# Early loads of three head pairs and the layout of the output weights, in attention followed by a gated feed-forward block

## The chip, the cores and the metric

The kernel runs on one core of a Trainium2 chip. The core has a matrix engine (TensorE, PE in the profile), a vector engine (VectorE, DVE), a scalar engine (ScalarE, ACT), a general engine (GpSimd, POOL) and an engine that only issues transfers (SyncE, SP). Each works through its own instructions in the order in which they were written. Transfers run on 16 DMA engines beside them. The metric is the device time of one execution, in microseconds (us).

## The reference

Attention over 8 batches of 12 heads, with 448 positions and head dimension 64, and then a feed-forward block with a gate over all 3584 tokens, with weights of 768 x 1536, 768 x 1536 and 1536 x 768:

```python
def _attn_ref(q, k, v):
    scale = 1.0 / np.sqrt(q.shape[-1])
    scores = scale * np.matmul(q, k.transpose(0, 1, 3, 2))
    scores = scores - np.max(scores, axis=-1, keepdims=True)
    attn = np.exp(scores)
    attn = attn / (np.sum(attn, axis=-1, keepdims=True) + 1e-09)
    return np.matmul(attn, v).astype(np.float32)

def _moe_ref(x, w_gate, w_val, w_out):
    g = x @ w_gate
    silu = g * (1.0 / (1.0 + np.exp(-g)))
    val = x @ w_val
    return (silu * val @ w_out).astype(np.float32)
```

The attention output, with its heads laid side by side, is the x of the feed-forward block. All inputs and the output are float32.

## The kernel before, in words

**Attention by pairs of heads.** There are 48 pairs, and the main loop runs over them in order (`pr`). `qk_half` computes the scores of half a pair, two tiles of 112 keys (or chunks) at a time (L199), and ScalarE turns each tile into exponentials E in fp16 (L206). The score tiles have two buffers in PSUM, so the score product of one tile waits until ScalarE is done with the tile two before it. `sums` (L237) and `pv` (L215) multiply E with ones and with the values for two pairs together, and `scaled` (L229) writes the product into X, the input of the feed-forward block.

**Queries and keys.** They must be turned so that the head dimension lies on partitions. Pair 0 is loaded by SyncE in fp32 (`load_qk0`, L110), cast to fp16 by VectorE and ScalarE (L153, L154) and turned by TensorE (`turn0`). The other pairs are loaded by GpSimd, whose DMA casts to fp16 on the way (`load_qk16`, L118). Pairs 1 to 10 are turned by TensorE straight from that tile (`turn`, L185), and VectorE copies the result out (L188). From pair 11 on (`NPE`), GpSimd copies the pair into another order (L156), and SyncE issues a DMA that transposes it (L159). The transpose of pair `pr + 3` is issued right behind the first half of the scores of pair `pr`. Values come in groups of three pairs (`load_v`, L127).

**Feed-forward in eight blocks.** A block has 384 or 512 tokens. `ffn1_steps` makes, for each of 12 column tiles, the gate product (L264 or L267, tile gp) and the value product (vp), with a tanh on ScalarE and two VectorE operations between them. `ffn2_steps` multiplies the result hts with the output weights: for each chunk of 128 tokens and each half of 384 output columns (`oh`), 12 matmuls sum over the 1536 inner rows into one PSUM tile op. ScalarE copies that into a staging tile osb (L320), of which there are three, and SyncE writes the finished chunk to the output with one DMA for each piece of contiguous positions, two to a chunk here (L332).

**The order.** Everything is written out by hand. Block 0 starts at pair 6 (`FIRST`); its feed-forward steps are spread over the loop by `ffn_run`, which takes steps from a list according to a time budget, so that score products, value products and feed-forward steps alternate on TensorE. The six steps of block 0's own output product are at the end of its list (`own`) and fall in pairs 11, 12 and 13, two steps to a pair. Blocks 1 and later mix the output steps of the block before them among their own.

**The weights.** GpSimd loads them, with a cast to fp16, in between the loads of q, k and v: table `wq` says at which pair. Gate and value weights come in three column pieces (384, 384 and 768 columns). The output weights come in three pieces of 512 rows, all 768 columns (`wo0` to `wo2`), one at pair 6 and two at pair 7. An output step needs all 1536 rows of its 384 columns.

Of the kernel before, what the change touches and what calls it, by code (L numbers as in the profile page):

```python
# [10 lines left out]
FP32 = mybir.dt.float32  # L11
FP16 = mybir.dt.float16
# [4 lines left out]
HS = 4096.0  # L17
# [10 lines left out]
def kernel(  # L28
# [60 lines left out]
        i = min(fb // 3, 2)  # L89
        return wgv[kind, i][:, cb, ds(fb * 128 - WSPL[i][0], 128)]  # L90

    wo = [consts.tile([128, NFB // 3, DM], FP16, name=f"wo{i}") for i in range(3)]

    raw = {}
    v16 = {}
# [7 lines left out]
        for _ in range(n):  # L103
            nc.tensor.matmul(wp[:], lhsT=warm[:, 0:128], rhs=warm[:], start=True, stop=True)

    def load_qk0():
        rq = raws.tile([P, 2, NC, D], FP32, tag="rq", bufs=RB)
        rk = raws.tile([P, 2, NC, D], FP32, tag="rk", bufs=RB)
        for dst, src in ((rq, q), (rk, k)):
            nc.sync.dma_start(dst[:], src[0, 0:2].rearrange("h (p c) d -> p h (c d)", c=NC))  # L110
        raw[0] = (rq[:], rk[:])

    def load_qk16(pr, n=2):
        q16 = raws.tile([P, 4, NC, D], FP16, tag="rq", bufs=RB, name="q16")
# [16 lines left out]

    def load_w(kind, i):
        if kind == "o":
            n = NFB // 3
            src = moe_w_out[i * n * 128 : (i + 1) * n * 128, :].rearrange("(f p) m -> p f m", p=128)
            dst = wo[i]
        else:
            src = (moe_w_gate if kind == "g" else moe_w_val)[:, ds(*WSPL[i])].rearrange(
                "(a p t) m -> t p a m", p=128, t=2
            )  # L140
            for t in range(2):
                nc.gpsimd.dma_start(wgv[kind, i][:, t::2, :], src[t])
            return
        nc.gpsimd.dma_start(dst[:], src)

    def prep(pr):
        rq, rk = raw[pr]
        if pr == 0 or pr >= NPE:
            qk16 = attp.tile([P, 2, NC, 2, D], FP16, tag="qk16", bufs=3)
            for t, src in enumerate((rq, rk)):  # L150
                dst = qk16[:, 1 - t].rearrange("p c h d -> p h c d")
                if pr == 0:
                    nc.vector.tensor_copy(dst[:, 0], src[:, 0])  # L153
                    nc.scalar.activation(dst[:, 1], src[:, 1], AF.Copy)  # L154
                else:
                    nc.gpsimd.tensor_copy(dst, src)  # L156
        qkT[pr] = attp.tile([128, 2 * NC, P], FP16, tag="qkT", name="qkT", bufs=5)
        if pr >= NPE:
            nc.sync.dma_start_transpose(  # L159
                qkT[pr][:], qk16[:].rearrange("p t c h d -> p (t c h d)")  # L160
            )
            return None

        def turn0():
            for t in range(2):
                tp = ps_s.tile([128, 2, 512], FP32, tag="s", name="tp")
                for c in range(NC):
                    for hx in range(2):
                        nc.tensor.matmul(
                            tp[ts(hx, 64), c // 2, ds(c % 2 * P, P)],  # L170
                            lhsT=qk16[:, 1 - t, c, hx],
                            rhs=ident[:],
                            start=True,
                            stop=True,
                        )
                dst = qkT[pr][:, ts(1 - t, NC)].rearrange("p (a c) q -> p a (c q)", a=2)
                nc.vector.tensor_copy(dst[:, 0], tp[:, 0, 0 : 2 * P])
                nc.scalar.activation(dst[:, 1], tp[:, 1, 0 : 2 * P], AF.Copy)

        def turn():  # L180
            tp = ps_f.tile([128, 2 * NC, 128], FP16, tag="f", name="tp")
            for t in range(2):
                for c in range(NC):
                    for hx in range(2):
                        nc.tensor.transpose(  # L185
                            tp[ts(hx, 64), (1 - t) * NC + c, 0:P], raw[pr][t][:, hx, c, :], ident[:]
                        )
            nc.vector.tensor_copy(qkT[pr][:], tp[:, :, 0:P])  # L188

        return turn if pr else turn0  # L190
# [71 lines left out]
    def mm(dst, lhsT, rhs, start, stop):  # L262
        if not tiled[0]:
            nc.tensor.matmul(dst, lhsT=lhsT, rhs=rhs, start=start, stop=stop)  # L264
            return
        for j in range(4):
            nc.tensor.matmul(  # L267
                dst[ts(j, 32), :], lhsT=lhsT[:, ts(j, 32)], rhs=rhs, start=start, stop=stop
            )

    def ffn1_steps(kk, c0, n, hts):
        for fb in range(NFB):
            gp = ps_f.tile([128, 512], FP32, tag="f")
            for cb in range(NCB):
                mm(
                    gp[:, 0:n],
                    lhsT=wslice("g", fb, cb),
                    rhs=X[kk][:, cb, ds(c0, n)],
                    start=(cb == 0),
                    stop=(cb == NCB - 1),  # L280
                )
            sg = fp.tile([128, 512], FP32, tag="sg")
            nc.scalar.activation(sg[:, 0:n], gp[:, 0:n], AF.Tanh, scale=0.5)  # L283
            yield NCB * n / 2400.0
            vp = ps_f.tile([128, 512], FP32, tag="f")
            for cb in range(NCB):
                mm(
                    vp[:, 0:n],
                    lhsT=wslice("v", fb, cb),
                    rhs=X[kk][:, cb, ds(c0, n)],  # L290
                    start=(cb == 0),
                    stop=(cb == NCB - 1),
                )
            t1 = fp.tile([128, 512], FP32, tag="t1")
            nc.vector.scalar_tensor_tensor(  # L295
                t1[:, 0:n], sg[:, 0:n], 1.0, gp[:, 0:n], ALU.add, ALU.mult
            )
            nc.vector.scalar_tensor_tensor(  # L298
                hts[:, fb, 0:n], t1[:, 0:n], 0.5 * HS, vp[:, 0:n], ALU.mult, ALU.mult
            )  # L300
            yield NCB * n / 2400.0

    def ffn2_steps(kk, c0, n, hts, last_block):
        for ch in range(n // 128):
            last = last_block and ch == n // 128 - 1
            for oh in range(2):
                if last or oh == 0:
                    osb = fp.tile([128, DM], FP32, tag="osb", bufs=3)
                parts = [(OH, OH // 2), (OH + OH // 2, OH // 2)] if last and oh else [(oh * OH, OH)]
                for m0, w in parts:  # L310
                    op = ps_f.tile([128, 512], FP32, tag="f")
                    for fb in range(NFB):
                        mm(
                            op[:, 0:w],
                            lhsT=hts[:, fb, ts(ch, 128)],
                            rhs=wo[fb // (NFB // 3)][:, fb % (NFB // 3), ds(m0, w)],
                            start=(fb == 0),
                            stop=(fb == NFB - 1),
                        )
                    nc.scalar.activation(osb[:, ds(m0, w)], op[:, 0:w], AF.Copy, scale=1.0 / HS)  # L320
                    if not last:
                        m0, w = 0, DM
                        if oh == 0:
                            continue
                    l0 = c0 + ch * 128
                    l = l0
                    while l < l0 + 128:
                        b, j = divmod(l, S)
                        c, p0 = divmod(j, P)
                        m = min(P - p0, l0 + 128 - l)  # L330
                        eng = nc.scalar if last and m < 64 else nc.sync
                        eng.dma_start(  # L332
                            out[ts(NB * kk + b, S), :].rearrange("(p c) m -> c p m", c=NC)[
                                c, p0 : p0 + m, ds(m0, w)
                            ],
                            osb[l - l0 : l - l0 + m, ds(m0, w)],
                        )
                        l += m
                yield NFB * OH / 2400.0

    def block(i):
        kk, odd = divmod(i, 2)
        c0, n = (384, 512) if odd else (0, 384)
        hts = hp_.tile([128, NFB, 512], FP16, tag="h")
        return ffn1_steps(kk, c0, n, hts), ffn2_steps(kk, c0, n, hts, i == B - 1), n

    with tc.manual_schedule():
        load_qk0()
        nc.vector.memset(warm[:], 0.0)
        nc.vector.memset(ones[:], 1.0)  # L350
        load_qk16(1, 1)
        make_identity(nc, ident)
        load_v(0, 0, 2)
        load_qk16(2, 1)
        load_v(0, 2)
        load_qk16(3, 1)
        load_qk16(4)
        load_v(1)
        dummy(6)
# [7 lines left out]
            3: [("qk", 10), ("V", 2), ("g", 2), ("v", 2)],  # L367
            4: [("qk", 12)],
            6: [("V", 3), ("o", 0)],
            7: [("o", 1), ("o", 2)],  # L370
        }

        def emit(item):
# [158 lines left out]
```

## Time and profile before

| | |
|---|---|
| time, median of 4 runs | 467.57 us (465.80 to 471.06) |
| the profiled execution's own time | 465.8 us |
| its span, first to last instruction | 463.8 us |
| TensorE matmul busy | 453.9 us (98%) |
| ScalarE busy | 243.2 us (52%) |
| VectorE busy | 236.9 us (51%) |
| GpSimd busy | 101.9 us (22%) |
| mean granted TensorE clock | 0.996 |
| read from HBM, written to it | 47.19 MB, 11.01 MB |

The busy time of TensorE is the union of its matmuls, whose ends are modelled and overlap: a long run of matmuls counts as busy throughout even where each waits a little for the one before. A row of the timeline reads: start, length, engine, line, operation, output <- inputs, number of instructions, and in brackets how long the engine was idle before it and what ended that. A row of the waits reads: who waited for whom, microseconds in total, number of times, the longest.

### The profile page before, as it was taken

The numbers are of one execution on the slowest core, as the hardware profiler recorded it, in microseconds if no ns is written. First come the engines' busy times: TensorE is split into PE (matmuls) and PEld (weight loads), VectorE is DVE, ScalarE is ACT, GpSimd is POOL, SyncE is SP. The second block draws the span as 40 slices with busy tenths as digits, with TensorE's granted clock in tenths as the row PEclk, the third lists the DMA queues.
The fourth block names the chain that finished last, engine by engine and source line by source line (L and its number), as shares of the span: only waits on it lengthen the run. The fifth ranks groups of instructions, "written<-read, shape, count | busy, mean of one in ns | idle before, by whom it ended". The sixth has DMA issues, their size and how long they took to land.

```text
span 463.8 us, 14131 instructions
## 1 busy us (share of the span) xinstructions
PE 453.9 (98%) x6367; PEld 228.0 (49%) x6367; DVE 236.9 (51%) x371; ACT 243.2 (52%) x353; POOL 101.9 (22%) x162
## 2 busy tenths in 40 slices
PE   7899989999999999999999999999999999999996
PEld 3345444444455555444455555444445556554454
DVE  2565763466764553655645635545456546334310
ACT  7887556656565555546455564546455552222222
POOL 8554407241350042202222040210200000000000
PEclk9899999999999999999999999999999999999999
DMA  9999999991994282861939675813513111101123
GB/s 142 197 199 209 174 185 197 188 166 30 110 124 62 63 112 42 131 94 28 140 40 108 95 109 95 116 31 75 90 17 55 37 37 35 36 2 34 35 68 102
DMA packets 78940, 44.23 MB, mean 95 GB/s; under 512 B 36640, under 2 KB 75424, under 8 KB 78880
## 3 DMA queue, kind: packets, MB, share of 16 engines
q0 software_dynamic: 39264, 23.37, 38.4%
q1 hardware_dynamic: 39520, 19.92, 24.6%
q8 instruction: 49, 0.80, 0.7%
q14 instruction: 11, 0.09, 0.1%
q10 hardware_dynamic: 96, 0.05, 0.0%
HBM read 47.19 MB, written 11.01 MB: 125 GB/s over the span
## 4 chain that ended last, share of the span: by engine, by line
PE 84%; DMA 13%; POOL 2%; issue 1%; ACT 0%; POOLq 0%
PE gp L267 15%; PE op L264 14%; PE vp L267 13%; PE op L267 10%; PE vp L264 9%; PE s L199 8%; PE acc L215 7%; PE gp L264 7%; DMA wo<-in_moe_w_out_dram 6%; DMA wg<-in_moe_w_gate_dram 5%; PE acc L237 4%; DMA q<-in_q_dram 2%; POOL q L118 1%; POOL k L118 0%; POOL vt L127 0%
## 5 line engine op out<-in xcount | busy, mean ns | idle before, releaser
L206 ACT ACTIVATE E<-s 112x896 f16<-112x896 f32 x192 | 164.8, 916 | 26.2 <-PE s L199 26.0
L283 ACT ACTIVATE sg<-gp 128x384 f32<-128x384 f32 (+1 forms) x96 | 52.3, 545 | 85.4 <-PE gp L267 54.7
L295 DVE SCALAR_TENSOR_TENSOR t<-sg,gp 128x384 f32<-128x384 f32 (+1 forms) x96 | 58.5, 610 | 64.3 <-ACT sg L283 64.2
L320 ACT ACTIVATE osb<-op 128x384 f32<-128x384 f32 (+1 forms) x57 | 27.7, 486 | 102.0 <-PE op L264 57.8
L267 PE MATMUL gp<-X,wg 128*32 128x512 f16 (+1 forms) x1416 | 78.1, 355 | 0.0
L252 DVE RECIPROCAL R<-ssb 128x112 f32<-128x112 f32 x92 | 73.1, 827 | 0.7
L298 DVE SCALAR_TENSOR_TENSOR hts<-t,vp 128x384 f16<-128x384 f32 (+1 forms) x96 | 59.6, 621 | 23.3 <-PE vp L267 7.9
L264 PE MATMUL op<-wo,hts 128*128 128x384 f16 (+1 forms) x408 | 68.7, 321 | 1.4 <-DMA wo<-in_moe_w_out_dram 1.4
L267 PE MATMUL vp<-X,wv 128*32 128x512 f16 (+1 forms) x1224 | 66.9, 353 | 0.0
L229 DVE TENSOR_TENSOR X<-acc,R 128x448 f16<-128x448 f32 x48 | 29.7, 624 | 66.4 <-PE acc L215 64.5
L264 PE MATMUL vp<-X,wv 128*128 128x384 f16 (+1 forms) x270 | 58.4, 352 | 0.0
L199 PE MATMUL s<-qkT 64*128 64x448 f16 x384 | 54.9, 357 | 2.4 <-ACT E L206 2.0
L264 PEld LDWEIGHTS <-hts 128*128 128x128 f16 x408 | 38.9, 98 | 29.7 <-issue 4.6
L267 PEld LDWEIGHTS <-wg 128*32 128x32 f16 x1416 | 37.8, 97 | 29.6
L267 PE MATMUL op<-wo,hts 128*32 128x384 f16 x1104 | 48.9, 326 | 0.0
L264 PE MATMUL gp<-X,wg 128*128 128x384 f16 (+1 forms) x222 | 47.4, 350 | 0.0
L215 PE MATMUL acc<-E,vt 112*32 112x448 f16 x768 | 45.5, 357 | 0.0
L267 PEld LDWEIGHTS <-wv 128*32 128x32 f16 x1224 | 32.7, 97 | 25.5
L127 POOL DMA_DIRECT2D vt<-in_v_dram x17 | 13.0, 763 | 145.5 <-PE acc L215 144.4
L264 PEld LDWEIGHTS <-wv 128*128 128x128 f16 x270 | 25.3, 98 | 26.9 <-issue 4.8
L267 PEld LDWEIGHTS <-hts 128*32 128x32 f16 x1104 | 29.5, 97 | 16.3
L156 POOL COPY qk<-q 112x512 f16<-112x512 f16 x37 | 22.9, 620 | 63.9 <-DMA qkT<-qk 47.8
(38 smaller groups left out, 199.2 us busy)
## 6 DMA issues: line engine op xcount, KB each, us to landing
vt<-in_v_dram POOLq DMA_DIRECT2D x15, 336.0 KB, 5.1
q<-in_q_dram POOLq DMA_DIRECT2D x22, 224.0 KB, 6.2
k<-in_k_dram POOLq DMA_DIRECT2D x22, 224.0 KB, 7.3
out_dram<-osb SPq DMA_DIRECT2D x7, 336.0 KB, 3.1
wo<-in_moe_w_out_dram POOLq DMA_DIRECT2D x3, 768.0 KB, 24.2
out_dram<-osb SPq DMA_DIRECT2D x8, 288.0 KB, 2.9
out_dram<-osb SPq DMA_DIRECT2D x8, 240.0 KB, 3.0
out_dram<-osb SPq DMA_DIRECT2D x8, 192.0 KB, 2.7
```

Source lines behind the costliest of these rows:

```text
L156: nc.gpsimd.tensor_copy(dst, src)
L199: nc.tensor.matmul(s[:, hx, 0:S], lhsT=t[ts(hx, 64)].rearrange("p c q -> p (c q)")[:, c * P : c * P + 128], rhs=t[ts(hx, 64), NC:, :].rear ...
L206: nc.scalar.activation(E[pr][:, c], s[0:P, :, 0:S], AF.Exp, scale=sm_scale)
L215: nc.tensor.matmul(acc[ts(j, 32), 0:S], lhsT=v16[g][:, 2 * r + j % 2, c, :].rearrange("p (d t) -> p t d", t=2)[:, t], rhs=E[p0 + j // 2][: ...
L229: nc.vector.tensor_tensor(X[kk][:, hp + t, ts(bb, S)], acc[:, 0:S], R[p0][:], ALU.mult)
L252: lambda i=i: nc.vector.reciprocal(rt[:, ts(i, P)], ssb[:, ts(i, P)]) for i in range(4)
L264: nc.tensor.matmul(dst, lhsT=lhsT, rhs=rhs, start=start, stop=stop)
L267: nc.tensor.matmul(dst[ts(j, 32), :], lhsT=lhsT[:, ts(j, 32)], rhs=rhs, start=start, stop=stop)
L283: nc.scalar.activation(sg[:, 0:n], gp[:, 0:n], AF.Tanh, scale=0.5)
L295: nc.vector.scalar_tensor_tensor(t1[:, 0:n], sg[:, 0:n], 1.0, gp[:, 0:n], ALU.add, ALU.mult)
L298: nc.vector.scalar_tensor_tensor(hts[:, fb, 0:n], t1[:, 0:n], 0.5 * HS, vp[:, 0:n], ALU.mult, ALU.mult)
L320: nc.scalar.activation(osb[:, ds(m0, w)], op[:, 0:w], AF.Copy, scale=1.0 / HS)
```

## The change

There are three edits.

1. **Pair 1.** `load_qk0` becomes `load_qk32(pr)`, and SyncE now loads pairs 0 and 1 in fp32. `prep(1)` has VectorE cast both tensors into a tile qk16 (two casts of 112 x 512), and `turn` takes pair 1 from there. GpSimd no longer issues the two loads of pair 1.
2. **Order of the first loads on GpSimd.** Before: pair 1, values of pair 0, pair 2, values of pairs 1 and 2, pair 3, pairs 4 and 5, values of group 1. After: pair 2, pair 3, all the values of group 0 in one transfer, pairs 4 and 5, values of group 1.
3. **Output weights.** Instead of three tiles of 512 rows x 768 columns there are two tiles of 1536 rows x 384 columns, one loaded at pair 6 and one at pair 7. Block 0 takes its output steps in another order: first all three chunks with the first half of the columns, then all three with the second half. Each of these six steps takes a staging tile of its own and writes its half of the columns with DMAs of its own. The other blocks keep their order and only address the weights anew.

```diff
-    wo = [consts.tile([128, NFB // 3, DM], FP16, name=f"wo{i}") for i in range(3)]
+    wo = [consts.tile([128, NFB, OH], FP16, name=f"wo{i}") for i in range(2)]
...
-    def load_qk0():
+    def load_qk32(pr):
         rq = raws.tile([P, 2, NC, D], FP32, tag="rq", bufs=RB)
         rk = raws.tile([P, 2, NC, D], FP32, tag="rk", bufs=RB)
         for dst, src in ((rq, q), (rk, k)):
-            nc.sync.dma_start(dst[:], src[0, 0:2].rearrange("h (p c) d -> p h (c d)", c=NC))
-        raw[0] = (rq[:], rk[:])
+            nc.sync.dma_start(dst[:], src[0, 2 * pr : 2 * pr + 2].rearrange("h (p c) d -> p h (c d)", c=NC))
+        raw[pr] = (rq[:], rk[:])
...
-            n = NFB // 3
-            src = moe_w_out[i * n * 128 : (i + 1) * n * 128, :].rearrange("(f p) m -> p f m", p=128)
+            src = moe_w_out[:, ts(i, OH)].rearrange("(f p) m -> p f m", p=128)
...
-        if pr == 0 or pr >= NPE:
+        if pr < 2 or pr >= NPE:
...
-                    nc.gpsimd.tensor_copy(dst, src)
+                    (nc.gpsimd if pr > 1 else nc.vector).tensor_copy(dst, src)
...
-                        nc.tensor.transpose(
-                            tp[ts(hx, 64), (1 - t) * NC + c, 0:P], raw[pr][t][:, hx, c, :], ident[:]
-                        )
+                        src = qk16[:, 1 - t, c, hx] if pr == 1 else raw[pr][t][:, hx, c, :]
+                        nc.tensor.transpose(tp[ts(hx, 64), (1 - t) * NC + c, 0:P], src, ident[:])
...
-    def ffn2_steps(kk, c0, n, hts, last_block):
-        for ch in range(n // 128):
-            last = last_block and ch == n // 128 - 1
-            for oh in range(2):
-                if last or oh == 0:
-                    osb = fp.tile([128, DM], FP32, tag="osb", bufs=3)
...
+    def ffn2_steps(kk, c0, n, hts, first, last_block):
+        chunks = range(n // 128)
+        if first:
+            steps = [(ch, oh) for oh in range(2) for ch in chunks]
+        else:
+            steps = [(ch, oh) for ch in chunks for oh in range(2)]
+        for ch, oh in steps:
+            last = first or (last_block and ch == n // 128 - 1)
+            if last or oh == 0:
+                osb = fp.tile([128, DM], FP32, tag="osb", bufs=3)
...
+                        rhs=wo[oh][:, fb, ds(m0 - oh * OH, w)],
...
-        load_qk0()
+        load_qk32(0)
+        load_qk32(1)
         nc.vector.memset(warm[:], 0.0)
         nc.vector.memset(ones[:], 1.0)
-        load_qk16(1, 1)
+        load_qk16(2, 1)
         make_identity(nc, ident)
-        load_v(0, 0, 2)
-        load_qk16(2, 1)
-        load_v(0, 2)
         load_qk16(3, 1)
+        load_v(0)
         load_qk16(4)
         load_v(1)
...
-            7: [("o", 1), ("o", 2)],
+            7: [("o", 1)],
```

More of the change, by code (lines that the diff above doesn't have):

```diff
@@ L301, in ffn1_steps @@
             yield NCB * n / 2400.0
-    def ffn2_steps(kk, c0, n, hts, last_block):
-        for ch in range(n // 128):
-            last = last_block and ch == n // 128 - 1
-            for oh in range(2):
-                if last or oh == 0:
-                    osb = fp.tile([128, DM], FP32, tag="osb", bufs=3)
[L309 to L339, printed above, removed]
@@ new lines, in ffn2_steps @@
+    def ffn2_steps(kk, c0, n, hts, first, last_block):
[8 more added lines that the diff above has]
+                osb = fp.tile([128, DM], FP32, tag="osb", bufs=3)
+            parts = [(OH, OH // 2), (OH + OH // 2, OH // 2)] if last and oh and not first else [(oh * OH, OH)]
+            for m0, w in parts:
+                op = ps_f.tile([128, 512], FP32, tag="f")
+                for fb in range(NFB):
+                    mm(
+                        op[:, 0:w],
+                        lhsT=hts[:, fb, ts(ch, 128)],
+                        rhs=wo[oh][:, fb, ds(m0 - oh * OH, w)],
+                        start=(fb == 0),
+                        stop=(fb == NFB - 1),
+                    )
+                nc.scalar.activation(osb[:, ds(m0, w)], op[:, 0:w], AF.Copy, scale=1.0 / HS)
+                if not last:
+                    m0, w = 0, DM
+                    if oh == 0:
+                        continue
+                l0 = c0 + ch * 128
+                l = l0
+                while l < l0 + 128:
+                    b, j = divmod(l, S)
+                    c, p0 = divmod(j, P)
+                    m = min(P - p0, l0 + 128 - l)
+                    eng = nc.scalar if last and m < 64 and not first else nc.sync
+                    eng.dma_start(
+                        out[ts(NB * kk + b, S), :].rearrange("(p c) m -> c p m", c=NC)[
+                            c, p0 : p0 + m, ds(m0, w)
+                        ],
+                        osb[l - l0 : l - l0 + m, ds(m0, w)],
+                    )
+                    l += m
+            yield NFB * OH / 2400.0
@@ L344, in block @@
         hts = hp_.tile([128, NFB, 512], FP16, tag="h")
-        return ffn1_steps(kk, c0, n, hts), ffn2_steps(kk, c0, n, hts, i == B - 1), n
+        return ffn1_steps(kk, c0, n, hts), ffn2_steps(kk, c0, n, hts, i == 0, i == B - 1), n
     with tc.manual_schedule():
-        load_qk0()
+        load_qk32(0)
+        load_qk32(1)
         nc.vector.memset(warm[:], 0.0)
         nc.vector.memset(ones[:], 1.0)
-        load_qk16(1, 1)
+        load_qk16(2, 1)
         make_identity(nc, ident)
-        load_v(0, 0, 2)
-        load_qk16(2, 1)
-        load_v(0, 2)
         load_qk16(3, 1)
+        load_v(0)
         load_qk16(4)
```

## The prediction

> **What bounds the kernel now.** The page's second part first.
>
> ```profile
> PE   7899989999999999999999999999999999999996
> PEclk9899999999999999999999999999999999999999
> DMA  9999999991994282861939675813513111101123
> ```
>
> A slice is 11.6 us. TensorE is full from the third slice to the last, so a stall of TensorE there costs its length, and a gain in the first 31 us is kept only if nothing later makes TensorE wait. DMA is full for nine slices, 104 us: until then transfers come when the queue gets to them, not when they are asked for. The second slice has a lower clock. The waits of TensorE are short:
>
> ```profile
> PE s L199 <- ACT E L206: 2.0, 4, 0.8
> PE op L264 <- DMA wo<-in_moe_w_out_dram: 1.4, 1, 1.4
> ...
> PE tp L185 <- DMA q<-in_q_dram: 0.4, 1, 0.4
> ...
> PE tp L185 <- DMA k<-in_k_dram: 0.2, 1, 0.2
> ```
>
> Windows of 3.41 us put the clock beside the work (length, busy, matmuls, granted clock, DMA share, GB/s):
>
> ```profile
> 10.85:14.26 3.41, 2.00 (x34) 1.00 1.40 184
> 14.26:17.67 3.41, 3.41 (x44) 0.50 1.44 198
> 65.45:68.87 3.42, 2.47 (x18) 1.00 1.19 156
> ```
>
> A window with TensorE busy for 2.00 us (59%) was followed by one at half clock, one with 2.47 us (72%) was not. Last, the timeline where block 0 projects:
>
> ```profile
> 66.45 1.46 PE L264 MATMUL op<-wo,hts 128*128 128x384 f16 x8
> 69.28 0.81 PE L264 MATMUL op<-wo,hts 128*128 128x384 f16 x4 [1.36 <-DMA wo<-in_moe_w_out_dram]
> 73.21 1.22 SPq L159 DMA_TRANSPOSE qkT<-qk  x1
> 74.48 1.04 SPq L332 DMA_DIRECT2D out_dram<-osb  x2
> 75.70 1.65 SPq L159 DMA_TRANSPOSE qkT<-qk  x1
> 80.01 1.07 SPq L332 DMA_DIRECT2D out_dram<-osb  x2
> 86.30 0.62 POOL L156 COPY qk<-q 112x512 f16<-112x512 f16 x1 [6.17 <-DMA qkT<-qk]
> 86.31 0.49 ACT L320 ACTIVATE osb<-op 128x384 f32<-128x384 f32 x1 [1.31 <-PE op L264]
> 88.86 0.55 PE L199 MATMUL s<-qkT 64*128 64x448 f16 x4
> ```
>
> Eight of the first step's twelve matmuls run on wo0 and wo1, and four wait 1.36 us for wo2. On SP a transpose (pair 14) goes out at 73.21, behind it the outputs of chunk 0, then pair 15's transpose, which lands at 86.15 (GpSimd's copy of pair 18 waits for it), then chunk 1's outputs, issued at 80.01 and 80.37, which land at 88.42 and 88.83.
>
> **Pair 1 and the order of the loads.** Gains: GpSimd issues two loads of 0.66 to 0.78 us less, and the two value loads become one, so pair 3 is issued at about 3.2 and 3.9 instead of 5.91 and 6.57. It lands at about 8.5 instead of 11.18 and 11.79, and the 0.6 us of waits at L185 go. ScalarE's idle time in front of E up to 19 us is 0.53, 0.56, 0.46 and 0.60 us. The first is that wait. The other three lie in the half-clock window, where `sums` took 1.30 us (0.94 elsewhere) and `pv` 1.29 (0.94). Without the wait the window before would be busier, and the drop probably goes: 0.5 + 1.2 = 1.7 us at most, if the drop goes; 0.5 if it stays.
>
> Costs: VectorE gets two casts of 112 x 512. Half that size took 0.39 us (L153), so one is 0.65 us by that row (0.78 doubled; 0.5 at best). VectorE is free from 5.58 to 7.27, which hides 1.3 us but for the start: the key tensor of pair 1 is fourth in SP's queue. Pair 0's two tensors landed at 3.58 and 4.28, 0.7 apart, which gives 5.7 alone and, beside GpSimd's loads, about 6.5. Its cast ends at 7.15, its transposes at 7.5 instead of 7.23, and the third score tile is 0.3 to 0.6 us late for ScalarE, whose E chain from 6.04 has no gap. I take 0.4. The start gains 1.3 us at most, 0.1 with the drop; I take 1.0. The values of group 0 are first used at 16.92 and land at about 10.5, as before: hidden, 6 us of cover. Cover gone, `pv` would wait.
>
> **Does the fp32 route relieve the DMA?** Pair 0's 448 KB moved at up to 337 GB/s, casting loads at about 200 GB/s written (400 read): 1.3 us of the engines for a pair in fp32, 1.1 us for its 224 KB with a cast. No work is saved. The Trainium skill (DMA: Bandwidth & Descriptors, "Issuing engines are not separate DMA queues") says that loads from SyncE and GpSimd share the same 16 engines and that only issue time is saved. By it the stream of loads gains nothing. But by the trace the engines were not full: values and pair 2 (112 KB each) landed at 7.11, 8.12 and 9.42, 1.0 to 1.3 us apart, and the pair 3 loads of the same size 0.6 apart. That is room of 1.6 us; I count 1.0 of it (0 to 1.6).
>
> **Output weights.** Bytes are the same, rows half as long. Gate pieces with such rows land 1.44 us per 288 KB, those with double rows 2.78 per 576: 0.05 us per 288 KB, so eight times that, 0.4 us, are lost, and one issue of 0.75 us on GpSimd is saved, which nobody waits for. The stream is then 1.0 - 0.4 = 0.6 us earlier behind the weights. The three pieces land between 56.06 and 69.24; the first half alone at about 62.5. The first step wants it at 66.45 less 1.0. The 1.36 us go. The second half is wanted by step 4 at about 75: hidden. The value weights that landed at 48.13 are wanted at 49.29 less 1.0, with 1.0 to spare: hidden as well. So TensorE would reach pair 14 some 2.4 us early.
>
> **The output stage, where a wait is added.** Six staging tiles are taken instead of three, from three buffers. Step 4, 5 and 6 copy into the buffers of steps 1, 2 and 3, so ScalarE waits for those outputs to land, and behind it on ScalarE stand the exponentials. On SP the outputs of step 1 stand behind pair 14's transpose, which waits for GpSimd's copies (SP waited 41 us in all for those before 110 us), and those of step 3 behind pair 15's. SP issues twelve outputs instead of six, 0.3 to 0.7 us each.
>
> Step 4: step 1's outputs follow the transpose, landed at 77.49 - 0.6, by some 1.5 us: 78.4. The copy is wanted at 79.49 - 2.4 = 77.1, and the scores of pair 13 tolerate about 78.4: nothing lost. Step 5: 80 or so against a tolerance of 82: nothing. Step 6 needs step 3's outputs. Pair 15's transpose landed 6.3 us after chunk 0's outputs (79.81); it follows steps 1 and 2 now, the same bytes in twice the rows: 79.8 - 0.6 + 0 to 1.5. Then step 3's two outputs, half of chunk 1's bytes, which landed up to 2.7 us after the transpose: 1.35 by bytes, 2.7 by rows. Together 86.15 - 0.6 + 0.6 + 1.7 = 87.9 (from 86.8 to 89.7).
>
> What does TensorE lose? Behind the copy on ScalarE come 0.4 us of its length and two exponentials of 0.87 us, and pair 14's second half needs the buffers of both: its last score product can go at 87.9 + 2.1 = 90.0. Before it went at 88.86 + 0.18 = 89.04. So the gain of 2.4 us is gone and about 1.0 is lost, the start's gain included, whatever it was. TensorE stands idle from about 86.5 to 90.0 but for one product. The clock: by the rows above, a window of 3.41 us with 59% of work was followed by a half-clock one. This idle time leaves one window with about 20%, or two with half. The Trainium skill (TensorE: Matmul & The Clock Gate, "Why this matters for your kernels") would only have an idle gap of over about 3 us return the clock to half, so by the rule it is at the edge: 0 or 1.7. By the row it is 3.41 / 2 = 1.7 us of lost work. I take the row. The sum is +1.0 + 1.7 = 2.7; with the transposes a little quicker, 2.3. I say +2.5.
>
> **The rivals.**
> 1. *The outputs land in time.* If pair 15's transpose takes 4.3 us as pair 14's did, not 6.3 behind outputs, or the buffers' halves are held apart, step 6 doesn't wait, and both gains stay: -1.36 - 1.0 = -2.4, with a part of the 1.8 us by which the median lies above the profiled run, which may be longer waits for wo2, up to -4. For it: pair 16's transpose took 3.3 us behind outputs. Against: the GpSimd copies show only one of three that fast in this stretch.
> 2. *The recycled buffers cost over 1%.* Transposes under full load took 11 to 16 us from issue (pairs 11 to 13). If pair 15's lands 3 us later, at 89.2, step 3's outputs land at 91; then TensorE loses 91 + 2.1 - 89.0 = 4.1 us and two windows at half clock, 3.4 less what overlaps: +6.5, 474.1. It decides from a landing at about 90.
> 3. *The edits don't reach the end:* the start is paced by E, wo2's wait moves to the next load, step 6 has just enough time: 0, 467.6. For it: the two amounts, 2.4 gained and 2.4 tolerated, are near each other.
>
> **How the numbers follow.** The sum is against the profiled execution: span 463.8, own time 465.8, the median 467.57. +2.5 makes a span of 466.3, own time 468.3, and 470.1 on the median, which is what is compared. Chances: the forecast 50%, rival 1 25%, rival 2 17%, rival 3 8%. The range takes the forecast (+0.8 to +4.5), the nearer end of rival 1 (-2.9) and most of rival 2 (+6.8): 464.7 to 474.4. One per cent, 4.7 us, is about what a measurement of this kernel can tell from no change. Faster by more: under half of rival 1, 0.11. Slower by more: nearly all of rival 2 and a quarter of the forecast, 0.29. Within: 0.60.
>
> **What would show it.** Right: no wait of op on wo; L185 no longer waits on q or k; ScalarE's osb copies of the fourth and sixth step wait for an output DMA; scores of pair 14 wait for E at about 86 to 90; then a window at half clock. The clock row around 14 us may be 1.00. Wrong: osb copies that wait only for TensorE, or the scores of pair 14 at about 86.4. The prediction falls if the drop at 14 us returns or moves between runs by more than the effect, or if output rows of 1536 bytes take as long as rows of 3072.

## The result, and the profile after

The changed kernel takes 465.96 us in the median of 43 runs (464.98 to 468.39), the one before 467.85 us in 64 runs beside it (464.84 to 471.06). The ratio is 0.9962 with a 95% interval of 0.9950 to 0.9975: 1.8 us faster, where 2.5 us slower were forecast. The fastest runs of both are nearly equal; the change mostly takes away the longer ones.

The profiled execution took 465.55 us with a span of 463.2 (before 465.8 and 463.8). The page's second part, for TensorE, its clock and the DMA:

```profile
PE   8899999999999999999999999999999999999996
PEclk9999999999999999999999999999999999999999
DMA  9999999991994373671948585813513111101123
```

The low clock in the second slice is gone. The rest of this part differs little, so the waits of TensorE come next:

```profile
PE s L197 <- ACT E L204: 1.8, 4, 0.4
PE wp L104 <- DVE ones L353: 1.2, 1, 1.2
PE tp L185 <- DVE qk L155: 0.6, 1, 0.6
PE tp L168 <- DVE qk L152: 0.5, 1, 0.5
PE acc L235 <- ACT E L204: 0.4, 1, 0.4
```

The wait of op for wo and those of L185 for q and k are gone. L185 now waits for the cast of pair 1 instead. The timeline of the start, ScalarE and VectorE:

```profile
6.86 1.73 ACT L204 ACTIVATE E<-s 112x896 f16<-112x896 f32 x2 [0.26 <-PE s L197]
7.12 0.65 DVE L155 CAST qk<-rq 112x512 f16<-112x512 f32 x1 [0.92 <-DMA rq<-in_q_dram]
...
8.51 0.43 DVE L155 CAST qk<-rk 112x512 f16<-112x512 f32 x1 [0.73 <-DMA rk<-in_k_dram]
...
10.64 1.73 ACT L204 ACTIVATE E<-s 112x896 f16<-112x896 f32 x2 [2.06 <-PE s L197]
```

The casts wait for the fp32 loads of pair 1, which land at 7.10 and 8.48 us. The chain of exponentials, which ran without a gap from 6.04 before, now stops for 2.06 us after two tiles. Block 0's first gate product starts at 32.16 instead of 31.24. From the timeline of block 0's output stage, with rows left out between these:

```profile
67.37 2.11 PE L262 MATMUL op<-wo,hts 128*128 128x384 f16 x12
72.08 1.22 SPq L158 DMA_TRANSPOSE qkT<-qk  x1
73.40 2.01 SPq L334 DMA_DIRECT2D out_dram<-osb  x4
75.59 1.73 SPq L158 DMA_TRANSPOSE qkT<-qk  x1
77.41 3.27 SPq L334 DMA_DIRECT2D out_dram<-osb  x4
78.94 0.49 ACT L322 ACTIVATE osb<-op 128x384 f32<-128x384 f32 x1 [0.48 <-PE op L262]
85.52 0.62 POOL L155 COPY qk<-q 112x512 f16<-112x512 f16 x1 [6.39 <-DMA qkT<-qk]
86.30 0.49 ACT L322 ACTIVATE osb<-op 128x384 f32<-128x384 f32 x1 [1.84 <-DMA out_dram<-osb]
88.26 0.55 PE L197 MATMUL s<-qkT 64*128 64x448 f16 x4
```

The twelve matmuls of the first step run through. Step 1's outputs do stand behind pair 14's transpose (72.08). They land at 77.72 and 78.20, so the copy of step 4, at 78.94, waits only for its product. The copy of step 6 waits 1.84 us for an output, as forecast. But the scores of pair 14's second half start at 88.26, 0.6 us earlier than before and with no wait in front of them. It was just in time: the last of these products goes at 88.46, and ScalarE had freed its buffer at 88.40.

**Three numbers for a profile.** They describe every profile of this study: G, the start of block 0's first gate product; W, from there to the scores of pair 15; and the rest. The rest is 370.4 to 370.5 us in all of them, before and after and in all variants. So whatever the edits do, they do it before pair 15, at about 93 us. W is 60.58 where TensorE waits for nothing on the way. Before: G 31.24, W 62.10. After: G 32.16, W 60.58. Between these two profiles the start lost 0.92 us, and the stretch behind it gained 1.52, of which 1.36 is the wait for wo2.

### The profile page after: what moved, and what is told of

Read it like the earlier page. It is cut to its first block, busy times and chain, and to the rows that moved or that the text cites. A ratio compares the mean times of both kernels' runs of the same rounds, so it can differ in the third digit from the quotient of the medians.

```text
span 463.2 us, 14146 instructions
## 1 busy us (share of the span) xinstructions
PE 455.0 (98%) x6367; PEld 228.4 (49%) x6367; DVE 237.9 (51%) x373; ACT 243.2 (52%) x353; POOL 99.9 (22%) x158
## 4 chain that ended last, share of the span: by engine, by line
PE 95%; ACT 2%; DMA 1%; SPq 0%; issue 0%; DVE 0%; ACTq 0%
PE gp L265 15%; PE op L262 14%; PE vp L265 13%; PE vp L262 11%; PE op L265 10%; PE s L197 10%; PE gp L262 9%; PE acc L213 9%; PE acc L235 4%; ACT E L204 2%; DMA rk<-in_k_dram 1%; PE tp L185 1%; PE wp L104 0%; SPq L110 0%; DVE qk L155 0%
## 5 line engine op out<-in xcount | busy, mean ns | idle before, releaser
L127 POOL DMA_DIRECT2D vt<-in_v_dram x16 | 12.4, 777 | 147.0 <-PE acc L213 146.4
```

## The experiments

Each was compared with runs of the kernel before on the same chip. "Time" is the ratio with its 95% interval. G, W and pair 15 come from one profiled execution each; the early version has two, and six runs for each of its two times. One more variant, six staging tiles instead of three, has no row: their pool would need 30 KB per partition, and 23.6 KB were left.

| kernel | G | W - 60.58 | pair 15 | time |
|---|---|---|---|---|
| before | 31.24 | 1.52 | 93.34 | 1 |
| before, second profile | 32.13 | 2.67 | 95.38 | |
| after | 32.16 | 0.00 | 92.74 | 0.9962 (0.9950 to 0.9975) |
| after, again | 32.90 | 0.00 | 93.48 | 0.9977 (0.9962 to 0.9992) |
| output weights alone | 32.06 | 1.43 | 94.07 | 0.9977 (0.9957 to 0.9996) |
| start alone | 32.45 | 2.00 | 95.03 | 0.9984 (0.9957 to 1.0011) |
| order of loads and output weights, no fp32 | 30.77 | 2.35 | 93.69 | 0.9981 (0.9962 to 1.0001) |
| after, a staging tile for each chunk | 33.12 | 0.00 | 93.70 | 0.9956 (0.9940 to 0.9972) |
| before, block 0 reads wo0 alone | 32.80 | 0.00 | 93.38 | 0.9957 (0.9939 to 0.9976) |
| early version | 30.64, 30.44 | 0.00, 0.04 | 91.22, 91.06 | 0.9927 (0.9899 to 0.9955), 0.9924 (0.9897 to 0.9952) |
| early version, recycled staging tiles | 29.91 | 6.39 | 96.88 | 1.0030 (1.0010 to 1.0049) |
| early version, fp32 pair 1 | 32.30 | 0.00 | 92.88 | 0.9959 (0.9945 to 0.9974) |
| the same, GpSimd's first load later | 30.84 | 0.00 | 91.42 | 0.9915 (0.9895 to 0.9935) |

**Output weights alone.** The change without its start: `load_qk0`, pair 1 by GpSimd, values as before.

```diff
-        load_qk32(0)
-        load_qk32(1)
+        load_qk0()
...
-        load_qk16(2, 1)
+        load_qk16(1, 1)
         make_identity(nc, ident)
-        load_qk16(3, 1)
-        load_v(0)
+        load_v(0, 0, 2)
+        load_qk16(2, 1)
+        load_v(0, 2)
+        load_qk16(3, 1)
```

> Only the output weights and block 0's step order are changed; the loads at the start are as before. Theory (the gain is the wait for the last third of the output weights, and the new start costs about 0.9 us): no wait of op for wo, ratio to before 0.993 to 0.995 (2.3 to 3.3 us less), that is more than the whole change. Rival (the gain comes from the start): 0.999 to 1.000. Rival of the prediction (recycled staging tiles take the gain back): TensorE arrives earlier than in the changed kernel, so the copy of step 6 waits 2.5 us or more and scores of pair 14 wait with it; ratio 0.998 to 1.003.

0.9977: less gain than my theory had (0.993 to 0.995), and just short of the range of the prediction's rival (0.998 to 1.003), which the interval overlaps. The wait for wo is gone, but another is there. Rows of the timeline of this kernel:

```profile
73.32 1.22 SPq L158 DMA_TRANSPOSE qkT<-qk  x1
...
74.59 2.00 SPq L335 DMA_DIRECT2D out_dram<-osb  x4
...
81.43 0.49 ACT L323 ACTIVATE osb<-op 128x384 f32<-128x384 f32 x1 [3.08 <-DMA out_dram<-osb]
82.78 0.37 PE L198 MATMUL s<-qkT 64*128 64x448 f16 x2 [0.62 <-ACT E L205]
...
83.59 0.37 PE L198 MATMUL s<-qkT 64*128 64x448 f16 x2 [0.44 <-ACT E L205]
```

The copy of step 4 waits 3.08 us for step 1's outputs, and the scores of pair 13 wait behind it. So the recycled tiles can reach TensorE, and not because it is early: step 1's product starts at 67.27 here and at 67.37 in the changed kernel. The outputs are late. Pair 14's transpose goes out at 73.32 instead of 72.08, and step 1's outputs land at 81.15 and 81.33 instead of 77.72 and 78.20.

**Start alone.** The change with the output weights in three pieces of rows and block 0's old order of steps.

```diff
-    wo = [consts.tile([128, NFB, OH], FP16, name=f"wo{i}") for i in range(2)]
+    wo = [consts.tile([128, NFB // 3, DM], FP16, name=f"wo{i}") for i in range(3)]
```

> Only the loads at the start are changed (pair 1 by SyncE in fp32, pairs 2 and 3 ahead of the values); output weights as before. Theory: block 0 begins 0.5 to 1 us later than before, but op's wait for wo shrinks by as much, so the end doesn't move: ratio 0.999 to 1.001. Rival (the gain comes from the start): 0.996 to 0.997.

0.9984 with 1 inside the interval, which holds the rival's 0.997 as well. In the profile G is 1.2 us later, more than the 0.5 to 1 expected, and op still waits 1.8 us for wo: the late start didn't shorten that wait as I had expected it to, since the weights were late too (70.93 instead of 69.24).

**Order and output weights, without fp32.** Pair 1 by GpSimd ahead of pair 2.

```diff
-        load_qk32(1)
+        load_qk16(1, 1)
```

> The changed kernel, but pair 1 is loaded by GpSimd with a cast, as before, ahead of pair 2. Theory: pair 1 lands at 5.5 and 6.1 instead of 7.1 and 8.5, so ScalarE's gap of 2 us in pair 0 goes, and the start is earlier than before: block 0 begins 0.5 to 1.5 us earlier than before; ratio to before 0.991 to 0.994, unless the staging tiles hold it at 0.996. Rival (the fp32 route is the gain): 0.997 to 1.000.

The start came out at the lower end of what was expected (G 30.77, 0.5 us earlier) and the time did not. The waits of TensorE say why:

```profile
PE s L198 <- ACT E L205: 2.7, 6, 0.4
PE vp L263 <- DMA wv<-in_moe_w_val_dram: 1.4, 1, 1.4
```

The last value weights landed at 50.45, where they had landed at 48.13 before, and the product that needs them was there earlier. The recycled tiles cost about 0.75 more: from pair 13 to pair 14 it took 7.57 us instead of 6.83 in the changed kernel. There too step 1's product starts where it did in the changed kernel (67.51), and its outputs land late, at 80.19 and 81.01. The ratio, 0.9981, lies in the rival's range, but its reason is not that fp32 loads start the kernel sooner: without them the start is earlier, and the value weights and the outputs land later.

**A staging tile for each chunk.** The two steps of a chunk share one, and each writes its half of the columns.

```diff
-            if last or oh == 0:
-                osb = fp.tile([128, DM], FP32, tag="osb", bufs=3)
+            if oh == 0 or (last and not first):
+                tiles[ch] = fp.tile([128, DM], FP32, tag="osb", bufs=3, name="osb")
+            osb = tiles[ch]
```

> The changed kernel, but the two steps of a chunk of block 0 share a staging tile and write its two halves, so that no copy waits for an output to land. Theory (in the changed kernel the late start leaves TensorE just the room, so the wait costs nothing when the start is late): no wait of osb copies for output DMAs; median within 0.15% of the changed kernel, at most 0.5 us better. Rival (recycled tiles cost in most runs): 0.8 us or more better than the changed kernel.

No copy waits for an output any more. The median is 465.73 us, beside 466.02 for the changed kernel on the same chip: 0.3 us. By the two ratios of the table it would be 1.0 us, but their intervals overlap. W is 60.58 in this profile and in both of the changed kernel, so in these the recycled tiles cost TensorE nothing.

**What the wait for wo2 is worth.** The kernel before, but block 0's output product reads the first third of the output weights for all its rows. It leaves out the other two thirds there, and with them the wait.

```diff
-                            rhs=wo[fb // (NFB // 3)][:, fb % (NFB // 3), ds(m0, w)],
+                            rhs=wo[0 if c0 == 0 and kk == 0 else fb // (NFB // 3)][:, fb % (NFB // 3), ds(m0, w)],
```

> The kernel before, but block 0's output steps read the first third of the output weights for all rows (the product of block 0 is left with wrong weights), so that they wait for the first third alone. It measures what the wait for the last third is worth. Theory (that wait is the gain): ratio 0.9955 to 0.997, as the whole change. Rival (the gain comes from elsewhere): 0.998 or more.

0.9957: taking the wait away alone gains as much as the whole change. The median falls by 2.6 us (467.37 to 464.73), more than the 1.36 us of the first profile. The second profile of the kernel before has the reason; this is its timeline of TensorE:

```profile
67.34 1.46 PE L264 MATMUL op<-wo,hts 128*128 128x384 f16 x8
71.32 0.81 PE L264 MATMUL op<-wo,hts 128*128 128x384 f16 x4 [2.51 <-DMA wo<-in_moe_w_out_dram]
```

> The kernel before, for a second profile. Theory (in most runs the wait for the last third of the output weights is longer than the 1.4 us of the first profile, or the start is later): block 0 between 31.2 and 33 us and op waits 1.5 to 4 us for wo, pair 15 at 60.6 us plus that wait behind it. Rival (the first profile is typical): 1.2 to 1.5 us.

2.51 us here: wo2 landed at 71.28, not at 69.24. That execution took 467.82 us, near the median; the first one, 465.8, is among the fastest quarter.

**The changed kernel again.**

> The changed kernel as it is, for the comparison on one chip: ratio to before 0.995 to 0.9975 in all theories; in its profile pair 15 begins between 92.0 and 93.5 us, and the first gate product at 31.5 to 32.5 if the fp32 loads of pair 1 land at 7 and 8.5 us again.

Pair 15 at 93.48, as expected. G is 32.90, later than expected, with the fp32 loads at 7.61 and 8.92, later than the 7 and 8.5 that the expectation assumed. W is 60.58 once more. Step 1's outputs had landed by 77.28.

**The early version.** All that the readings so far name as a limit is taken away: pair 1 by GpSimd, pairs 2 and 3 ahead of the values, output weights in halves, a staging tile for each chunk, and the values of group 2 behind the last gate and value weights:

```diff
-            3: [("qk", 10), ("V", 2), ("g", 2), ("v", 2)],
+            3: [("qk", 10), ("g", 2), ("v", 2), ("V", 2)],
```

> Pair 1 by GpSimd as before, pairs 2 and 3 ahead of the values, output weights in halves, one staging tile for each chunk in block 0, and the values of group 2 loaded behind the last gate and value weights. Theory (the start, the value weights at 48 to 50 us, the staging tiles and the output weights take turns as the limit, and none of the four holds now): block 0 begins at about 30.8 and pair 15 at about 91.3 us in the profile, 2 us earlier than in the profile of before; ratio to before 0.992 to 0.995. Rival (something else limits, the time is that of the changed kernel): 0.996 to 0.998.

> The early version with one staging tile for each chunk, again, since few of its runs counted the first time. Ratio to before 0.9905 to 0.994; block 0 at 30.5 to 31 us, pair 15 at 60.58 us behind it (the least that any profile shows), 91.1 to 91.6.

0.9927 and 0.9924, with medians of 463.71 and 463.49 us: faster than both kernels. G and pair 15 come within 0.2 us of what was expected, all on the early side.

**The recycled tiles with an early start.** The early version with the change's way of taking staging tiles.

```diff
-            if oh == 0 or (last and not first):
-                tiles[ch] = fp.tile([128, DM], FP32, tag="osb", bufs=3, name="osb")
-            osb = tiles[ch]
+            if last or oh == 0:
+                osb = fp.tile([128, DM], FP32, tag="osb", bufs=3)
```

> The early version (pair 1 by GpSimd, pairs 2 and 3 ahead of the values, output weights in halves, values of group 2 behind the last gate and value weights) with the recycled staging tiles of the change, six from three buffers, instead of one for each chunk. TensorE arrives about 2 us earlier than in the changed kernel, so this is the case that the prediction reckoned with. Theory: copies of steps 4 and 6 wait for outputs and the scores of pairs 13 and 14 with them; pair 15 begins 0.7 to 2 us later than with a tile for each chunk (91.2), at 91.9 to 93.2; ratio to before 0.994 to 0.9965. The prediction as it stood: pair 15 at about 94.3 and a window at half clock after it: ratio 0.999 to 1.002. Rival (the recycled tiles cost nothing even then): 91.0 to 91.5 and 0.992 to 0.9935.

TensorE is as early here as the prediction had reckoned with, and this kernel is the slowest: 1.0030, median 468.92. My theory at that time had the cost far too small, and the prediction's number was the nearer one. Timeline of this kernel, SP, ScalarE and TensorE:

```profile
73.38 1.22 SPq L158 DMA_TRANSPOSE qkT<-qk  x1
...
74.66 3.00 SPq L335 DMA_DIRECT2D out_dram<-osb  x4
...
81.61 0.49 ACT L323 ACTIVATE osb<-op 128x384 f32<-128x384 f32 x1 [5.41 <-DMA out_dram<-osb]
82.00 1.72 ACT L205 ACTIVATE E<-s 112x896 f16<-112x896 f32 x2
82.96 0.56 PE L198 MATMUL s<-qkT 64*128 64x448 f16 x2 [2.94 <-ACT E L205]
...
85.87 3.94 PE L263 MATMUL op<-wo,hts 128*128 128x384 f16 x12
```

Step 1's outputs are issued behind pair 14's transpose at 74.66 and land at 79.21 and 81.50. The copy of step 4 waits for them, ScalarE's exponentials wait behind the copy, and the scores of pair 13 wait for those. Then twelve matmuls take 3.94 us where they had taken 2.12. Windows of 3.41 us of this kernel, TensorE alone (length, busy, matmuls, granted clock, DMA share, GB/s), say why:

```profile
79.37:82.78 3.41, 0.65 (x4) 1.00 1.35 217
82.78:86.19 3.41, 2.98 (x22) 0.50 1.33 152
86.19:89.61 3.42, 3.42 (x12) 0.50 1.34 222
89.61:93.02 3.41, 3.41 (x50) 1.00 1.24 244
```

One window with 0.65 us of work is followed by two at half clock, worth 3.4 us. With the wait of 2.94 that makes about the 6.39 in the table.

**The fp32 route by itself.** The early version with `load_qk32(1)` as in the change.

> The same, but with pair 1 loaded by SyncE in fp32 as in the change; nothing else differs. Theory (the fp32 loads land at 7.5 and 8.9 instead of 5.7 and 6.3, and cost the start about 2 us): block 0 at 32.1 to 33.1, ratio to before 0.9945 to 0.997, and 0.0025 to 0.005 above the version with pair 1 by GpSimd. Rival (the fp32 route costs nothing in the median): within 0.001 of it.

G is 32.30 instead of 30.44 to 30.64, and the ratio 0.9959 instead of 0.9924 and 0.9927: about 0.0033, or 1.5 us in time (1.9 to 2.2 between the medians) and 1.8 in G. Loading pair 1 in fp32 costs about what the new order of the other loads gains. The same edit has a second effect: with two loads less on GpSimd, pair 14's transpose goes out at 71.45 here, and at 73.54 and 75.37 in the two profiles of the early version.

**Why the fp32 loads are late.** The same kernel, with GpSimd held back before its first load by twelve clears and by the making of the identity, which stood behind that load:

```diff
+        make_identity(nc, ident)
+        hold = consts.tile([112, 112], FP16, name="hold")
+        for _ in range(12):
+            nc.gpsimd.memset(hold[:], 0.0)
         load_qk16(2, 1)
-        make_identity(nc, ident)
```

> The early version with pair 1 in fp32 and a staging tile for each chunk, but GpSimd first clears a scratch tile twelve times (about 2 us) before it issues its first load, so that the fp32 loads of pair 1 have the DMA engines to themselves. Theory (pair 1 is late because its loads share the engines with GpSimd's): pair 1 lands at 4.9 to 6.0 instead of 7.4 and 8.7, and ScalarE's gap in pair 0 is under 0.7 us instead of 2.9. Rival (the fp32 loads are slow by themselves or by their place in SP's queue): they land at 6.8 or later and the gap stays over 1.5 us. The time says less, since all of GpSimd's loads are 2 us late: ratio to before 0.992 to 1.000.

GpSimd issues its first load at 4.17 instead of 1.3 us, and pair 1 lands at 5.89 and 6.43 instead of 7.4 and 8.7; the gap of ScalarE is 1.12 us instead of 2.92. The landings are at or near the theory's, so sharing the engines with GpSimd's loads accounts for the lateness. The gap lies between the two expectations, but what is left of it is not the loads': the same 1.12 us stands in "order and output weights, without fp32" and in the first profile of the early version, where pair 1 comes by GpSimd and lands at 5.6 to 6.3. In these three profiles TensorE's clock record begins at about 10 us, and its first matmuls run at half speed. In the second profile of the early version, with the clock up at 5.1, ScalarE has no such gap. The ratio, 0.9915, is the lowest of the study, though all of GpSimd's loads start 2.9 us later. The intervals of this and the early version overlap, so which of the two is faster stays open.

## Why the prediction was wrong

**Two terms failed: the start's gain and the landing of step 3's outputs.** The forecast's 2.5 was 1.0 of lost time and 1.7 of half clock, less a little. The 1.0 came from one landing: step 3's outputs at 87.9, and 2.1 us later, at 90.0, the last score product of pair 14. They landed at 86.19, below the whole range given (86.8 to 89.7), and that product went at 88.46, 0.6 us earlier than before. The 2.1 us from that landing to the product held within 0.2. The 1.7 needed a TensorE that stands idle, because it is 2.4 us ahead. It was 0.6 us ahead and did not wait.

**Why the start gained nothing.** The prediction put the second of pair 1's fp32 loads at "5.7 alone and, beside GpSimd's loads, about 6.5", took 0.4 us for it and 1.0 us as the gain of the start. The two landed at 7.10 and 8.48, and in four other profiles with this start at 7.4 to 8.9. Its bound from below had been 0.1 us of gain; a loss was left out, though the next paragraph has the two streams on the same engines. GpSimd's loads were slowed as well: pair 2 landed at 6.94 and 8.30. How much was lost is less certain than the 0.92 us of the first two profiles:

| loads at the start | G in four profiles | mean |
|---|---|---|
| as before | 31.24, 32.06, 32.13, 32.80 | 32.06 |
| as in the change | 32.16, 32.45, 32.90, 33.12 | 32.66 |
| the change's order, pair 1 by GpSimd | 29.91, 30.44, 30.64, 30.77 | 30.44 |

The first profile of before is the earliest of its four. A gain of 1.0 is not there. The means differ by 0.6, a loss, and the two rows overlap. The fp32 route costs 2.2 us by the last two rows, which do not overlap. A slow clock at the start is not the reason: in two profiles with the fp32 loads (the change with a tile for each chunk, the early version with fp32) the clock came up at 5.3 and 5.6 us, though it fell again at 8.7 and 9.1, and ScalarE's gap was 3.12 and 2.92 us all the same.

**The mechanism that was to cost 2.5 us is real, and what spared the changed kernel was the time at which its outputs landed.** Five profiles have recycled tiles:

| kernel | step 1 starts | pair 14's transpose issued | step 1's outputs landed by | cost |
|---|---|---|---|---|
| after | 67.37 | 72.08 | 78.20 | 0 |
| after, again | 68.11 | 71.14 | 77.28 | 0 |
| output weights alone | 67.27 | 73.32 | 81.33 | 1.43 |
| order and output weights, no fp32 | 67.51 | 73.77 | 81.01 | 0.75 |
| early version, recycled | 65.12 | 73.38 | 81.50 | 6.39 |

At step 4 the forecast of 78.4 and "nothing lost" was right for the change. The third and fourth row have TensorE where the first has it, and pay, because their outputs land 3 us later. The fourth differs from the changed kernel in the route of pair 1 alone (its value weights cost it another 1.4, earlier); its pair 14 keys, for which the transpose waits, landed at 73.07 instead of 71.39. So the edit that took the gain from the start also brought pair 14's transpose and the outputs behind it forward. The prediction had this as 0.6 us in the stream of loads; it had not seen that step 4 hangs on it. Two things stay open: why the late outputs also took longer from issue to landing (4.6 to 6.6 us instead of 4.2 to 4.4), and why the start alone, with the weights in three pieces, did not bring the transpose forward (74.89). With TensorE 2 us earlier still (the last row) the chain ran as described: outputs behind a transpose, copy, exponentials, scores, half clock, for 5 to 6 us. It did so at step 4, where the prediction had seen no cost. At step 6 the changed kernel had 0.06 us of room, 0.15 in its second profile: that nothing waited there is luck.

**Other terms of the sum.**
- Step 3's outputs: forecast 87.9, measured 85.81 and 86.19. They came 0.4 and 0.8 us behind pair 15's transpose (85.38), not 1.7. The fear of the shorter rows was not borne out there.
- The wait for wo2: mis-sized for the median. It was 1.36 us in the first profile, 2.51 in the second, 2.6 in the median by the kernel that needs wo0 alone. The prediction allowed for that under its first rival only and compared with the median all the same.
- The stream of loads: forecast 0.6 us earlier behind the weights. The second half landed at 69.57, wo2 had landed at 69.24; but pair 14's tensors behind it landed at 70.23 and 71.39 instead of 71.10 and 72.51, about 1 us earlier. By the Trainium skill's rule (DMA: Bandwidth & Descriptors, "Issuing engines are not separate DMA queues") nothing was to be gained there. At the start the rule fits: the two streams slowed each other.
- The first half: forecast 62.5, measured 60.65, wanted at 67.37. Right. Edits hidden as said: the values of group 0 landed at 11.34, wanted at 18.19.
- The last value weights "with 1.0 to spare": 49.29 less 1.0 less 48.13 is 0.16, so the 1.0 stands only with the room counted above. They landed at 48.59 and nothing waited, but with an earlier start they were the next limit, 1.4 us.
- VectorE's casts: forecast 0.65 each, measured 0.65 and 0.43, right.
- The clock: the row taken as a rule, half clock behind a window with 59% of work, does not hold alone. In the second profile of before, a window with 1.88 us of work in 3.42 (55%, from 69.78) was followed by one at full clock. One with 19% was followed by two at half clock in the early version with recycled tiles; the 1.7 us was too small by half for that case. The other rule weighed there (the Trainium skill, TensorE: Matmul & The Clock Gate, "Why this matters for your kernels", over about 3 us of idle) agrees with both: the waits were 2.51 and 2.94 us, the second at its edge. It does not explain the window of 59%, in which no gap was over 0.9 us. In the changed kernel no such window came.
- What a measurement can tell: the interval of the result is 0.25% wide, so 0.4% stands out from no change, where the prediction had put the limit at about one per cent.
- One of the three idle times laid to the half-clock window at the start ends at 18.55, behind that window's end at 17.67.

**The rivals.** The first one, that both gains stay, gave -2.4 to -4 and was nearest to the result, in part by luck: the start's gain did not come, and the wait for wo2 was worth more than its 1.36. Its reason, faster transposes, was not the cause: pair 15's took 9.79 us from its issue, nearly as long as the 10.45 before. The second gave +6.5 by an output landing 3 us late; what it described was seen in the early version with recycled tiles, at step 4. The third, 0, had two things right: a start that gains nothing, and a step 6 with just enough time.

**What stays open.** Times of the same kernel differ by 1.7 to 6.8 us from run to run, and one profile shows one of them. The table's differences of G under 1 us (30.77 against 31.24, or 32.16 against 32.90 for the same kernel) are no larger than that. How often each of the waits occurs in runs without a profile can only be read from medians.

## What to carry to other kernels

A gain that makes an engine early is worth nothing until the next thing on its way is early too: before adding gains, list for each later step when its input lands and when a buffer comes free, and see what happens if the estimate of the start is wrong by 2 us in either direction. A sum that turns on the difference of two estimates of that size has two outcomes, not one with a range. An edit that moves a load to another queue also moves what stands behind it on the old one: follow both. When a staging buffer is released by a DMA that is queued behind something else, let the parts of one tile share it, as in the variant with a tile for each chunk, at no cost in memory.

## What the runs showed of the hardware

- Loads from SyncE and GpSimd that were under way together slowed each other: with both from the start, two fp32 loads landed at 7.4 and 8.7, with GpSimd's first issue 2.9 us later at 5.9 and 6.4.
- One window of 3.41 us with TensorE busy for 0.65 us was followed by two windows at half clock; one with 1.88 us was followed by full clock, one with 2.00 us by half. So the busy share of a window does not decide alone.
- In the changed kernel TensorE ran at half speed until about 12.4 us, though the clock row shows 9 from the first slice: four score matmuls took 0.94 us at 6.26 and 0.55 later. The trace's first record of a clock change is at 12.5 us in that profile, and at 4.0 in the first profile of before. The row tells nothing ahead of its first record.
